# Query weights loaded by groups of four heads instead of whole at the start, with x, w1 and the output in the matching layout: a decode attention and MLP block on one core

## The chip, the core and the metric

The kernel runs on one core of one Trainium2 chip. The core has a matrix engine (TensorE: PE, with its weight loads shown as PEld), a vector engine (DVE), a scalar engine (ACT), GpSimd (POOL), and a synchronisation engine (SP) whose queue issues most of the DMA transfers; 16 DMA engines move the data between HBM and the core's SBUF. The metric is device time in microseconds. The kernel before takes 1960.25 us, the median of three runs that lie between 1960.19 and 1960.85.

## The reference

One token is decoded: layer norm, attention with 32 heads over a cache of 32,768 positions, a residual, a second layer norm, and an MLP. All inputs are bf16.

```
B, Sq, D = 1, 1, 640
H, Sk, Dh = 32, 32768, 192        # Dff = 1536
q = (x @ wq).reshape(B, Sq, H, Dh)                      # wq: 640 x 6144
scores = einsum("bhqd,bhkd->bhqk", q, k_cache) * Dh ** -0.5
p = softmax(scores)
o = einsum("bhqk,bhkd->bhqd", p, v_cache)
A = o.reshape(B, Sq, H * Dh) @ wo                       # wo: 6144 x 640

h  = x + A(layernorm(x))
h2 = h + relu(layernorm(h) @ w1) @ w2                   # w1: 640 x 1536, w2: 1536 x 640
```

The two caches are 403 MB each, wq and wo 7.9 MB each, w1 and w2 2.0 MB each. Every byte is read once.

## The kernel before

**Streaming the caches.** For each head, K and V are loaded in four pieces of 8,192 positions. A piece is a tile of 128 partitions with 64 consecutive positions in each, so each partition receives one row of 24,576 bytes (64 x 192 x 2). K tiles come from kpool and V tiles from vpool, with three buffers each. All these loads are issued on SP's queue (load_part, line 128), in the order of the program; an issue waits until the tile's buffer has been read for the last time. The last piece of the last head is cut into three loads (40, 16 and 8 positions per partition) to shorten the end; the very last K piece takes a wo buffer and the very last V piece a tile of its own, v_end.

**A chunk.** Each piece is worked on in chunks of 32 positions per partition, eight chunks to a head (the index c). Of a chunk's positions, 12 or 16 are scored on DVE (multiply with the spread query, line 287, and sum, line 290). The other 20 or 16 are scored on PE: transposes(g) turns K (line 252) and ACT copies it out of PSUM (line 256), and scores_pe(g) multiplies with the query as columns (line 267). ACT takes the exponentials (lines 272 and 300). pv(g-1) multiplies the chunk before with V, into one PSUM tile for the whole head (line 317). The order on each engine is the order in which the program is written (a manual schedule); around the chunks it fits, by the value of c, the loads of the next pieces (the even c), a load of wo for two heads (c = 1), the finishing of the head before (den_mm, den_rec, o_scale, o_turn at c = 0 and 1), the projection of the last pair of heads (project, line 363, c = 2) and the query of the next head (q_spread, c = 5).

**The query.** wq is loaded ahead of everything, in three loads (load_wq, line 108): two of them borrow a vpool tile and one a kpool tile. The contraction index is split as (p c): partition p holds the five rows 5p to 5p + 4 of wq, whole, so the rows that are moved are 24,576 bytes (two of wq's rows) or 12,288 bytes. Behind them stand, on SP's queue, K and V of the first piece, the first wo load and K of the second piece. q_rows() (line 213) then computes the queries of all heads in 12 blocks of 512 columns, five products each, into q_all; the buffers taken by wq are free when it has ended. Per head, q_spread copies its 192 values from q_all to a row (line 219), spreads them over the partitions by a product with ones (line 221), and makes the columns for scores_pe (line 227).

**The layout of x, h and the output.** They follow wq's split: x is loaded as 128 partitions of five consecutive values (x_b, line 98, on ACT's queue). project and the second product of the MLP (line 435) write the same layout, so they take every fifth column of wo and w2 as weights (n:D:DT). w1 is loaded in the same split, in rows of 15,360 bytes, and its product takes every twelfth column (line 428). The output y is written as 128 rows of five values (line 440).

**The end.** After the last loads of K and V come those of w1 and w2 (load_w, line 146). Then the last head is finished, projected, added to x, normalised, and goes through the MLP.

Of the kernel before, what the change touches and what calls it, by code (L numbers as in the profile page):

```python
# [13 lines left out]
def kernel(  # L14
# [12 lines left out]
    nc = tc.nc  # L27
    P = nc.NUM_PARTITIONS

    Bsz, Sq, D = A_x.shape  # L30
    _, H, Sk, Dh = A_k_cache.shape
    HDh = H * Dh
# [7 lines left out]
    FT = Dff // P  # L40
    JL = 64
    J = 32
    assert Sk % (P * JL) == 0 and 2 * Dh == 3 * P and H % 2 == 0 and HDh % 512 == 0

# [24 lines left out]
    const = ctx.enter_context(tc.tile_pool(name="const", bufs=1))  # L71
    kpool = ctx.enter_context(tc.tile_pool(name="kpool", bufs=3))
    vpool = ctx.enter_context(tc.tile_pool(name="vpool", bufs=3))
    wop = ctx.enter_context(tc.tile_pool(name="wop", bufs=2))
    qbp = ctx.enter_context(tc.tile_pool(name="qbp", bufs=2))
    tsb = ctx.enter_context(tc.tile_pool(name="tsb", bufs=2))
# [10 lines left out]
    def mm_bank(shape, dtype, name):  # L87
        return mps.tile(shape, dtype, tag="mm", name=name)

    k_hd = A_k_cache.rearrange("b h s d -> (b h) s d")  # L90
    v_hd = A_v_cache.rearrange("b h s d -> (b h) s d")

    wq_view = A_wq.rearrange("(p c) n -> p c n", p=P)
    wo_view = A_wo.rearrange("(g p b) n -> g p b n", p=P, b=3)


    x_b = const.tile([P, DT], bf16)
    nc.scalar.dma_start(out=x_b[:], in_=A_x.rearrange("b s (p c) -> (b s p) c", p=P))

    wq_t = {}  # L100
    wo_t = {}
    kt_t = {}
    vt_t = {}

    def load_wq(pool, tag, c0, c1):
        t = pool.tile([P, JL * Dh], bf16, tag=tag, name=tag)
        v = t[:, 0:(c1 - c0) * HDh].rearrange("p (c n) -> p c n", n=HDh)
        nc.sync.dma_start(out=v, in_=wq_view[:, c0:c1, :])
        for c in range(c0, c1):
            wq_t[c] = v[:, c - c0, :]  # L110

    def load_wo(pr):
        t = wop.tile([P, 3 * D], bf16, tag="wo", name="wo")
        t = t[:].rearrange("p (b n) -> p b n", n=D)
        nc.sync.dma_start(out=t, in_=wo_view[pr])
        wo_t[pr] = t

    def load_part(ld, src, pool, tag, name, parts=None):
        h, k0, jl = loads[ld]
        if ld < len(loads) - 1:  # L120
            t = pool.tile([P, JL * Dh], bf16, tag=tag, name=name)
        elif name == "kt":
            t = wop.tile([P, 3 * D], bf16, tag="wo", name=name)
        else:
            t = v_end
        rows = src[h, k0:k0 + P * jl, :].rearrange("(p j) d -> p (j d)", p=P)
        for j0, j1 in parts or [(0, jl)]:
            nc.sync.dma_start(out=t[:, j0 * Dh:j1 * Dh], in_=rows[:, j0 * Dh:j1 * Dh])
        return t
# [10 lines left out]
    def load_w(name, view, pool, tag, cuts):  # L140
        n, N = view.shape[1], view.shape[2]
        assert n * N <= JL * Dh
        t = pool.tile([P, JL * Dh], bf16, tag=tag, name=tag)
        v = t[:, 0:n * N].rearrange("p (c n) -> p c n", n=N)
        for c0, c1 in zip(cuts[:-1], cuts[1:]):
            nc.sync.dma_start(out=v[:, c0:c1], in_=view[:, c0:c1])
        for c in range(n):
            w_t[name, c] = v[:, c, :]

    assert (JL * Dh) // HDh == 2 and DT == 5  # L150
    load_wq(vpool, "vt", 0, 2)
    load_wq(vpool, "vt", 2, 4)
    load_wq(kpool, "kt", 4, 5)


    ident_b = const.tile([P, P], bf16)
# [16 lines left out]
    o_pair = [[const.tile([2, 2 * Dh], f32, name=f"o_pair{i}_{k}") for k in range(2)] for i in range(2)]  # L173
    attT = aps.tile([P, DT], f32, name="attT")
    x_col = const.tile([P, DT], f32)
    q_all = const.tile([1, HDh], bf16)
    v_end = const.tile([P, chunks[-1][4] * Dh], bf16)

    def layernorm_col(col, tag):
        st = small.tile([P, 2], f32, tag=f"st_{tag}", name="st")  # L180
# [18 lines left out]
        return xn  # L199

    with tc.manual_schedule():
        nc.vector.tensor_copy(out=x_col[:], in_=x_b[:])
        xnT = layernorm_col(x_col, "ln1")

        qb_t = {}
        qm_t = {}

        def q_rows():
            for i in range(HDh // 512):
                qps = tps.tile([P, 4, P], f32, tag="tp", name="tp")  # L210
                qps = qps[:].rearrange("p a b -> p (a b)")[0:1, :]
                for c in range(DT):
                    nc.tensor.matmul(qps, lhsT=xnT[:, c:c + 1], rhs=wq_t[c][:, i * 512:(i + 1) * 512],  # L213
                                     start=(c == 0), stop=(c == DT - 1))
                (nc.vector.tensor_copy if i % 2 else nc.scalar.copy)(out=q_all[0:1, i * 512:(i + 1) * 512], in_=qps)  # L215

        def q_spread(h):
            r = rows_e[h % 2]
            nc.scalar.copy(out=r[0:1, Dh:2 * Dh], in_=q_all[0:1, h * Dh:(h + 1) * Dh])  # L219
            qbps = mm_bank([P, Dh + 12], f32, "qbps")  # L220
            nc.tensor.matmul(qbps[:, 0:Dh], lhsT=ones_row[:], rhs=r[0:1, Dh:2 * Dh], start=True, stop=True)  # L221

            i = Dh
            for b in range(3):
                for e in range(2):
                    for off in ((1 - 0) * Dh + b * (2 * P - Dh), b * (2 * P - Dh)):
                        nc.tensor.matmul(qbps[:, i:i + 1], lhsT=r[0:1, off + e:off + 2 * P:2],  # L227
                                         rhs=ones_row[0:1, 0:1], start=True, stop=True)
                        i += 1
            qb = qbp.tile([P, Dh], bf16, name="qb")  # L230
            nc.scalar.copy(out=qb[:], in_=qbps[:, 0:Dh])
            qm = qbp.tile([P, 12], bf16, name="qm")
            nc.scalar.copy(out=qm[:], in_=qbps[:, Dh:Dh + 12])
            qb_t[h], qm_t[h] = qb, qm
# [6 lines left out]
        def transposes(g):  # L241
            h, c, ld, c0, jc, jp = chunks[g]
            kt = kt_t[ld]
            NB = jp * Dh // (2 * P)

            kT = tsb.tile([P, NBM, 2 * P], bf16, name="kT")
            for b0 in range(0, NB, 4):
                nb = min(4, NB - b0)
                tp = tps.tile([P, 4, P], f32, tag="tp", name="tp")
                for b in range(nb):  # L250
                    off = (c0 + jc - jp) * Dh + (b0 + b) * 2 * P
                    nc.tensor.transpose(out=tp[:, b, :], in_=kt[:, off:off + 2 * P].bitcast(f32), identity=ident_f[:])  # L252
                if g == G - 1:
                    nc.vector.tensor_copy(out=kT[:, b0:b0 + nb, :], in_=tp[:, 0:nb, :].bitcast(bf16))
                else:
                    nc.scalar.copy(out=kT[:, b0:b0 + nb, :], in_=tp[:, 0:nb, :].bitcast(bf16))  # L256
            kT_t[g] = kT
# [101 lines left out]
        def project(pr):  # L359
            oT, wo = oT_t.pop(pr), wo_t.pop(pr)  # L360
            for b in range(3):
                for n in range(DT):
                    nc.tensor.matmul(attT[:, n:n + 1], lhsT=wo[:, b, n:D:DT], rhs=oT[:, b:b + 1],
                                     start=(pr == 0 and b == 0 and n == 0),
                                     stop=(pr == H // 2 - 1 and b == 2 and n == DT - 1), skip_group_check=True)

        load_k(0)
        load_v(0)
        q_rows()
        q_spread(0)  # L370
        for g in range(ENDS[0]):
            h, c, ld, c0, jc, jp = chunks[g]
            if c0 == 0 and g > 0:
                load_k(ld)
                load_v(ld)
            if c == 1 and h % 2 == 0:
                load_wo(h // 2)
            transposes(g)
            if g > 0:
                pv(g - 1)  # L380
            scores_pe(g)
            sc = scores_dve(g)
            if c == 0 and h > 0:
                den_mm(h - 1)
                den_rec(h - 1)
                o_scale(h - 1)
            if c == 1 and h > 0:
                o_turn(h - 1)
            if c == 2 and h > 0 and h % 2 == 0:
                project(h // 2 - 1)  # L390
            if c == 5 and h + 1 < H:
                q_spread(h + 1)
            exp_dve(g, sc)
# [2 lines left out]
            load_k(ld)  # L396
        for ld in range(len(loads) - NEND, len(loads)):
            load_v(ld)
        load_w("w1", B_w1.rearrange("(p c) n -> p c n", p=P), kpool, "kt", [0, DT])
        load_w("w2", B_w2.rearrange("(p f) n -> p f n", p=P), vpool, "vt", [0, FT // 2, FT - 2, FT])  # L400
        transposes(ENDS[0])
        pv(ENDS[0] - 1)
# [29 lines left out]
        yps = ops.tile([P, DT], f32, tag="o_ps", name="yps")  # L432
        for f in range(FT):
            for n in range(DT):
                nc.tensor.matmul(yps[:, n:n + 1], lhsT=w_t["w2", f][:, n:D:DT], rhs=h1T[:, f:f + 1],  # L435
                                 start=(f == 0 and n == 0), stop=(f == FT - 1 and n == DT - 1),
                                 skip_group_check=True)
        y = small.tile([P, DT], bf16, tag="y", name="y")
        nc.vector.tensor_add(out=y[:], in0=h_col[:], in1=yps[:])
        nc.sync.dma_start(out=out.rearrange("b s (p c) -> (b s p) c", p=P), in_=y[:])  # L440


# [28 lines left out]
```

## Time and profile before

| quantity | value |
|---|---|
| median of three runs | 1960.25 us |
| the profiled execution, its own time | 1960.25 us |
| its span, first to last instruction | 1958.4 us |
| HBM read | 824.97 MB, 421 GB/s over the span |
| mean granted TensorE clock | 0.861 of full speed |
| PE / DVE / ACT busy, share of the span | 82% / 81% / 50% |
| queue q1 (loads issued by SP), share of 16 DMA engines | 98.8% |
| first chunk's first product with K, start | 37.24 us |
| x landed, after its issue | 10.2 us |
| out landed, after its issue | 2.8 us |

How to read it. Times within the execution are counted from its first instruction. Busy shares are averages over the whole span. The groups of instructions give an engine's line, operation, tiles and shapes, then the total busy time and the mean time of one in ns, and then the engine's idle time ahead of them with what ended it. In the waits, a line names the engine and line that waited, what it waited for, the total, the number of waits and the longest. In the stretches, a line gives the stretch, its length, the busy time of PE, PEld, DVE, ACT and POOL with the number of instructions, the granted TensorE clock, the busy share of the DMA engines and the rate in GB/s. The chain of waits is followed back from the last instruction: at each step to what released it, or to the instruction ahead of it on its engine.

### The profile page before, as it was taken

The page shows a single profiled execution, that of the slowest core. Times are in us where ns is not written, and L with a number is a line of the kernel's source. Part 1 is how long each engine was busy: PE and PEld are TensorE (multiplying, and loading weights), DVE is VectorE, ACT ScalarE, POOL GpSimd, SP SyncE. Part 2 cuts the span into 40 slices and gives each one's busy share as a digit, 9 for nine tenths or more (in the row PEclk, how much of TensorE's full clock was granted, in tenths as well). Part 3 has the DMA queues.
Part 4 walks back from the last instruction along what each step waited for, and adds up shares of the span by engine and source line. Part 5 has one row for each costly group of instructions (what it writes and reads, how often), then busy time and mean ns, then how long its engine had stood idle before and what let it go on. Part 6 is the DMA issues. An engine that isn't in the chain of part 4 may idle for free.

```text
span 1958.4 us, 35516 instructions
## 1 busy us (share of the span) xinstructions
PE 1603.5 (82%) x15578; PEld 1098.4 (56%) x15578; DVE 1583.7 (81%) x913; ACT 984.2 (50%) x2068; POOL 0.7 (0%) x6
## 2 busy tenths in 40 slices
PE   5888888888888888888887888788788887887887
PEld 2555555555555555555565655556555555555555
DVE  3897887888788888888887888788888878788885
ACT  2554545545555545454554545454555545455553
POOL 0000000000000000000000000000000000000000
PEclk9888888888888888898888888888888888889888
DMA  9999999999999999999999999999999999999996
GB/s 408 427 430 427 429 428 428 429 427 429 427 429 428 429 429 428 429 427 428 428 429 428 429 426 429 428 429 428 428 429 427 429 425 429 425 426 429 422 418 241
DMA packets 41338, 827.25 MB, mean 422 GB/s; under 512 B 4832, under 2 KB 4832, under 8 KB 8032
## 3 DMA queue, kind: packets, MB, share of 16 engines
q1 hardware_dynamic: 41040, 824.99, 98.8%
q8 instruction: 122, 2.00, 0.4%
q14 instruction: 32, 0.26, 0.0%
q10 hardware_dynamic: 144, 0.00, 0.0%
HBM read 824.97 MB, written 0.00 MB: 421 GB/s over the span
## 4 chain that ended last, share of the span: by engine, by line
DMA 70%; DVE 19%; PE 9%; issue 1%; ACT 0%; DVEq 0%; SPq 0%; ACTq 0%
DMA kt<-in_A_k_cache_dram 69%; DVE pr L287 11%; DVE sc L290 8%; PE o_ps L317 4%; PE tp L252 3%; DMA kt<-in_A_wq_dram 1%; PE sp L267 1%; PE tp L213 1%; DVE o_pair L340 0%; ACT kT L256 0%; PE h1ps L428 0%; PE den L323 0%; PE yps L435 0%; DVE rec L329 0%; DVE rec L330 0%
## 5 line engine op out<-in xcount | busy, mean ns | idle before, releaser
L287 DVE TENSOR_TENSOR pr<-kt,qb 128x1536 f32<-128x1536 bf16 (+1 forms) x384 | 775.4, 2019 | 225.1 <-DMA kt<-in_A_k_cache_dram 216.7
L256 ACT COPY kT<-tp 128x1024 bf16<-128x1024 bf16 (+1 forms) x898 | 816.5, 989 | 277.4 <-PE tp L252 270.6
L252 PE MATMUL tp<-ident_f,kt 128*128 128x128 f32 x3462 | 585.4, 336 | 305.4 <-DMA kt<-in_A_k_cache_dram 294.4
L290 DVE TENSOR_REDUCE sc<-pr 128x8 f32<-128x1536 f32 (+1 forms) x384 | 774.0, 2016 | 31.9 <-DVE pr L287 1.4
L252 PEld LDWEIGHTS tp<-ident_f,kt 128*128 128x128 f32 x3462 | 508.6, 176 | 322.8 <-issue 298.6
L317 PE MATMUL o_ps<-vt,pB 128*2 128x384 bf16 x2304 | 483.3, 362 | 3.1 <-DMA vt<-in_A_v_cache_dram 3.1
L317 PE MATMUL o_ps<-vt,pA 128*2 128x384 bf16 x1788 | 333.7, 327 | 0.0
L317 PEld LDWEIGHTS <-pB 128*2 128x2 bf16 x2308 | 189.0, 90 | 248.4 <-issue 137.4
L272 ACT ACTIVATE pB<-sp 128x20 bf16<-128x20 f32 (+2 forms) x258 | 47.8, 185 | 484.9 <-PE sp L267 484.9
L267 PEld LDWEIGHTS <-kT 128*128 128x128 bf16 x6924 | 192.7, 97 | 85.5 <-issue 84.1
L317 PEld LDWEIGHTS <-pA 128*2 128x2 bf16 x1788 | 151.5, 85 | 145.5 <-issue 7.6
L267 PE MATMUL sp<-qm,kT 128*128 128x2 bf16 x6924 | 214.7, 164 | 1.1 <-ACT kT L256 1.1
L300 ACT ACTIVATE pA<-sc 128x12 bf16<-128x12 f32 (+2 forms) x257 | 53.9, 210 | 115.0 <-DVE sc L290 114.9
L329 DVE TENSOR_REDUCE rec<-den 128x1 f32<-128x20 f32 x32 | 5.7, 179 | 68.7 <-PE den L323 68.7
L272 ACT ACTIVATION_READ_ACCUMULATOR pB<-sp 128x1 f32 x258 | 50.2, 195 | 0.0
L300 ACT ACTIVATION_READ_ACCUMULATOR pA<-sc 128x1 f32 x257 | 49.0, 190 | 0.0
L341 ACT ACTIVATE o_pair<-o_ps,rec 2x192 f32<-2x192 f32 x32 | 18.8, 589 | 32.7 <-DVE o_pair L340 32.7
L353 PE MATMUL oT_ps<-ident_f,o_pair 2*128 2x1 f32 x192 | 24.1, 247 | 0.9 <-DVE o_pair L340 0.6
L227 PEld LDWEIGHTS <-row_e 1*128 1x128 bf16 x384 | 13.6, 92 | 17.9 <-issue 17.9
L353 PEld LDWEIGHTS oT_ps<-ident_f,o_pair 2*128 2x128 f32 x192 | 22.6, 186 | 1.6 <-DVE o_pair L340 1.0
L221 PE MATMUL qbps<-row_e,ones_row 1*128 1x192 bf16 x32 | 7.6, 238 | 18.4 <-ACT row_e L219 17.2
L215 DVE CAST q_all<-tp 1x512 bf16<-1x512 f32 x6 | 4.1, 678 | 20.0 <-PE tp L213 20.0
(55 smaller groups left out, 169.7 us busy)
## 6 DMA issues: line engine op xcount, KB each, us to landing
kt<-in_A_k_cache_dram SPq DMA_DIRECT2D x127, 3072.0 KB, 33.1
vt<-in_A_v_cache_dram SPq DMA_DIRECT2D x127, 3072.0 KB, 30.5
wo<-in_A_wo_dram SPq DMA_DIRECT2D x16, 480.0 KB, 31.2
vt<-in_A_wq_dram SPq DMA_DIRECT2D x2, 3072.0 KB, 13.5
kt<-in_A_k_cache_dram SPq DMA_DIRECT2D x1, 1920.0 KB, 26.4
vt<-in_A_v_cache_dram SPq DMA_DIRECT2D x2, 960.0 KB, 19.2
kt<-in_B_w_dram SPq DMA_DIRECT2D x1, 1920.0 KB, 17.7
kt<-in_A_wq_dram SPq DMA_DIRECT2D x1, 1536.0 KB, 20.2
```

Source lines behind the costliest of these rows:

```text
L213: nc.tensor.matmul(qps, lhsT=xnT[:, c:c + 1], rhs=wq_t[c][:, i * 512:(i + 1) * 512], start=(c == 0), stop=(c == DT - 1))
L227: nc.tensor.matmul(qbps[:, i:i + 1], lhsT=r[0:1, off + e:off + 2 * P:2], rhs=ones_row[0:1, 0:1], start=True, stop=True)
L252: nc.tensor.transpose(out=tp[:, b, :], in_=kt[:, off:off + 2 * P].bitcast(f32), identity=ident_f[:])
L256: nc.scalar.copy(out=kT[:, b0:b0 + nb, :], in_=tp[:, 0:nb, :].bitcast(bf16))
L267: nc.tensor.matmul(sp[:, 4 * i + b:4 * i + b + 2], lhsT=kT[:, 3 * i + b, e:2 * P:2], rhs=qm[:, 4 * b + 2 * e:4 * b + 2 * e + 2], start=(i ...
L272: nc.scalar.activation(out=pB[:, 0:JP], in_=sp[:, 0:JP], func=F.Exp, scale=SCALE, accum_out=dsums[:, h, 2 * c + 1:2 * c + 2])
L287: nc.vector.tensor_tensor(out=pr[:, 0:j1 - j0, :], in0=kt[:, (c0 + j0) * Dh:(c0 + j1) * Dh].rearrange("p (j d) -> p j d", d=Dh), in1=qb[:] ...
L290: nc.vector.reduce_sum(out=sc[:, j0:j1], in_=pr[:, 0:j1 - j0, :], axis=mybir.AxisListType.X)
L300: nc.scalar.activation(out=pA[:, 0:JD], in_=sc[:, 0:JD], func=F.Exp, scale=SCALE, accum_out=dsums[:, h, 2 * c:2 * c + 1])
L317: nc.tensor.matmul(o[:], lhsT=p, rhs=vt[:, (c0 + j) * Dh:(c0 + j + 2) * Dh], start=first, stop=last)
L341: nc.scalar.activation(out=dst[1][:, p0:p1, :], in_=src[:, 1], func=F.Copy, scale=s[0:2, 1:2])
L353: nc.tensor.matmul(ps[:, b:b + 1], lhsT=src[i][:, b * P:(b + 1) * P], rhs=ident_f[0:2, i:i + 1], start=(i == 0), stop=(i == 1))
```

## The change

wq is no longer loaded whole ahead of everything. It is loaded in eight loads of four heads each (QG = 4) into a pool of its own with two buffers: the first ahead of the loop, each other one at c = 3 of the third head of the group before. The contraction index is split as (c p): partition p holds the rows p, 128 + p, 256 + p, 384 + p and 512 + p, and of each the 768 columns of the group. So a load has 640 rows of 1,536 bytes. q_rows(h) computes one head's query, five products of 192 columns, at c = 4 of the head before, and ACT copies it from PSUM into the row that q_spread reads; q_all and the copy in q_spread go.

The layout of x, h and the output follows the new split. x is loaded as five rows of 128 values and turned on PE. project and the second MLP product take 128 consecutive columns as weights. w1 is loaded in 640 rows of 3,072 bytes; its product still takes every twelfth column. The output is turned on PE, copied, and written as five rows of 128 values. The last K piece and the last V piece use buffers of wq's pool. The SBUF that all this takes is the same.

```diff
+    wqp = ctx.enter_context(tc.tile_pool(name="wqp", bufs=2))
-    wq_view = A_wq.rearrange("(p c) n -> p c n", p=P)
+    wq_view = A_wq.rearrange("(c p) n -> p c n", p=P)
-    x_b = const.tile([P, DT], bf16)
-    nc.scalar.dma_start(out=x_b[:], in_=A_x.rearrange("b s (p c) -> (b s p) c", p=P))
+    x_row = const.tile([DT, P], bf16)
+    nc.scalar.dma_start(out=x_row[:], in_=A_x.rearrange("b s (c p) -> (b s c) p", p=P))
-    def load_wq(pool, tag, c0, c1):
-        t = pool.tile([P, JL * Dh], bf16, tag=tag, name=tag)
-        v = t[:, 0:(c1 - c0) * HDh].rearrange("p (c n) -> p c n", n=HDh)
-        nc.sync.dma_start(out=v, in_=wq_view[:, c0:c1, :])
-        for c in range(c0, c1):
-            wq_t[c] = v[:, c - c0, :]
+    def load_wq(gq):
+        t = wqp.tile([P, DT * QG * Dh], bf16, tag="wq", name="wq")
+        t = t[:].rearrange("p (c n) -> p c n", c=DT)
+        nc.sync.dma_start(out=t, in_=wq_view[:, :, gq * QG * Dh:(gq + 1) * QG * Dh])
+        wq_t[gq] = t
...
-        if ld < len(loads) - 1:
-            t = pool.tile([P, JL * Dh], bf16, tag=tag, name=name)
-        elif name == "kt":
-            t = wop.tile([P, 3 * D], bf16, tag="wo", name=name)
+        if ld == len(loads) - 1:
+            pool, tag, size = wqp, "wq", DT * QG * Dh
         else:
-            t = v_end
+            size = JL * Dh
+        t = pool.tile([P, size], bf16, tag=tag, name=name)
...
-    load_wq(vpool, "vt", 0, 2)
-    load_wq(vpool, "vt", 2, 4)
-    load_wq(kpool, "kt", 4, 5)
+    load_wq(0)
...
-        nc.vector.tensor_copy(out=x_col[:], in_=x_b[:])
+        xps = mm_bank([P, DT], bf16, "xps")
+        nc.tensor.transpose(out=xps[:], in_=x_row[:], identity=ident_b[0:DT, 0:DT])
+        nc.vector.tensor_copy(out=x_col[:], in_=xps[:])
...
-        def q_rows():
-            for i in range(HDh // 512):
-                qps = tps.tile([P, 4, P], f32, tag="tp", name="tp")
-                qps = qps[:].rearrange("p a b -> p (a b)")[0:1, :]
-                for c in range(DT):
-                    nc.tensor.matmul(qps, lhsT=xnT[:, c:c + 1], rhs=wq_t[c][:, i * 512:(i + 1) * 512],
-                                     start=(c == 0), stop=(c == DT - 1))
-                (nc.vector.tensor_copy if i % 2 else nc.scalar.copy)(out=q_all[0:1, i * 512:(i + 1) * 512], in_=qps)
+        def q_rows(h):
+            gq, hh = divmod(h, QG)
+            wq = wq_t[gq]
+            qps = mm_bank([1, Dh], f32, "qps")
+            for c in range(DT):
+                nc.tensor.matmul(qps[:], lhsT=xnT[:, c:c + 1], rhs=wq[:, c, hh * Dh:(hh + 1) * Dh],
+                                 start=(c == 0), stop=(c == DT - 1))
+            r = rows_e[h % 2]
+            nc.scalar.copy(out=r[0:1, Dh:2 * Dh], in_=qps[:])
         def q_spread(h):
             r = rows_e[h % 2]
-            nc.scalar.copy(out=r[0:1, Dh:2 * Dh], in_=q_all[0:1, h * Dh:(h + 1) * Dh])
...
-                    nc.tensor.matmul(attT[:, n:n + 1], lhsT=wo[:, b, n:D:DT], rhs=oT[:, b:b + 1],
+                    nc.tensor.matmul(attT[:, n:n + 1], lhsT=wo[:, b, n * P:(n + 1) * P], rhs=oT[:, b:b + 1],
...
-        q_rows()
+        q_rows(0)
...
+            if c == 3 and h % QG == QG - 2 and h + 2 < H:
+                load_wq(h // QG + 1)
...
+            if c == 4 and h + 1 < H:
+                q_rows(h + 1)
...
-        load_w("w1", B_w1.rearrange("(p c) n -> p c n", p=P), kpool, "kt", [0, DT])
+        load_w("w1", B_w1.rearrange("(c p) n -> p c n", p=P), kpool, "kt", [0, DT])
...
-                nc.tensor.matmul(yps[:, n:n + 1], lhsT=w_t["w2", f][:, n:D:DT], rhs=h1T[:, f:f + 1],
+                nc.tensor.matmul(yps[:, n:n + 1], lhsT=w_t["w2", f][:, n * P:(n + 1) * P], rhs=h1T[:, f:f + 1],
...
-        y = small.tile([P, DT], bf16, tag="y", name="y")
-        nc.vector.tensor_add(out=y[:], in0=h_col[:], in1=yps[:])
-        nc.sync.dma_start(out=out.rearrange("b s (p c) -> (b s p) c", p=P), in_=y[:])
+        y_col = small.tile([P, DT], f32, tag="y_col", name="y_col")
+        nc.vector.tensor_add(out=y_col[:], in0=h_col[:], in1=yps[:])
+        ytp = mm_bank([DT, P], f32, "ytp")
+        nc.tensor.transpose(out=ytp[:], in_=y_col[:], identity=ident_f[:])
+        y_row = small.tile([DT, P], bf16, tag="y_row", name="y_row")
+        nc.vector.tensor_copy(out=y_row[:], in_=ytp[:])
+        nc.sync.dma_start(out=out.rearrange("b s (c p) -> (b s c) p", p=P), in_=y_row[:])
```

More of the change, by code (lines that the diff above doesn't have):

```diff
@@ L42 @@
     J = 32
-    assert Sk % (P * JL) == 0 and 2 * Dh == 3 * P and H % 2 == 0 and HDh % 512 == 0
+    QG = 4
+    assert Sk % (P * JL) == 0 and 2 * Dh == 3 * P and H % QG == 0 and H % 2 == 0
     full = [(JL, [(J, 20), (J, 16)])] * (Sk // (P * JL))
@@ L103 @@
     vt_t = {}
-    def load_wq(pool, tag, c0, c1):
-        t = pool.tile([P, JL * Dh], bf16, tag=tag, name=tag)
-        v = t[:, 0:(c1 - c0) * HDh].rearrange("p (c n) -> p c n", n=HDh)
-        nc.sync.dma_start(out=v, in_=wq_view[:, c0:c1, :])
-        for c in range(c0, c1):
-            wq_t[c] = v[:, c - c0, :]
+    def load_wq(gq):
[3 more added lines that the diff above has]
+        wq_t[gq] = t
     def load_wo(pr):
-        t = wop.tile([P, 3 * D], bf16, tag="wo", name="wo")
-        t = t[:].rearrange("p (b n) -> p b n", n=D)
-        nc.sync.dma_start(out=t, in_=wo_view[pr])
+        t = wop.tile([P, 3, D], bf16, name="wo")
+        nc.sync.dma_start(out=t[:], in_=wo_view[pr])
         wo_t[pr] = t
@@ L148, in load_w @@
             w_t[name, c] = v[:, c, :]
-    assert (JL * Dh) // HDh == 2 and DT == 5
-    load_wq(vpool, "vt", 0, 2)
-    load_wq(vpool, "vt", 2, 4)
-    load_wq(kpool, "kt", 4, 5)
+    load_wq(0)
     ident_b = const.tile([P, P], bf16)
@@ L175 @@
     x_col = const.tile([P, DT], f32)
-    q_all = const.tile([1, HDh], bf16)
-    v_end = const.tile([P, chunks[-1][4] * Dh], bf16)
     def layernorm_col(col, tag):
@@ L248, in transposes @@
                 nb = min(4, NB - b0)
-                tp = tps.tile([P, 4, P], f32, tag="tp", name="tp")
+                tp = tps.tile([P, 4, P], f32, name="tp")
                 for b in range(nb):
```

## The prediction

> **What bounds the kernel now.** I read the page first, then the waits of the SP queue, the stretches, the end of the chain of waits and the groups of instructions. The page (engine: busy us, share, instructions; 40 slices; queues):
>
> ```profile
> span 1958.4 us, 35516 instructions
> ...
> PE 1603.5 (82%) x15578; PEld 1098.4 (56%) x15578; DVE 1583.7 (81%) x913; ACT 984.2 (50%) x2068; POOL 0.7 (0%) x6
> ...
> DMA  9999999999999999999999999999999999999996
> GB/s 408 427 430 427 429 428 428 429 427 429 427 429 428 429 429 428 429 427 428 428 429 428 429 426 429 428 429 428 428 429 427 429 425 429 425 426 429 422 418 241
> ...
> q1 hardware_dynamic: 41040, 824.99, 98.8%
> q8 instruction: 122, 2.00, 0.4%
> ```
>
> Every slice but the last moves data at one rate while no engine passes 82%: the load stream of queue q1 is the bound. Next, whether that stream can run dry (releaser: total us, times, longest; then the issues with KB and us from issue to landing):
>
> ```profile
> SPq L128 <- PE o_ps L317: 1172.8, 125, 12.4
> SPq L128 <- DVE pr L287: 602.0, 126, 12.1
> ```
>
> ```profile
> kt<-in_A_k_cache_dram SPq DMA_DIRECT2D x127, 3072.0 KB, 33.1
> vt<-in_A_v_cache_dram SPq DMA_DIRECT2D x127, 3072.0 KB, 30.5
> ...
> vt<-in_A_wq_dram SPq DMA_DIRECT2D x2, 3072.0 KB, 13.5
> ...
> kt<-in_A_wq_dram SPq DMA_DIRECT2D x1, 1536.0 KB, 20.2
> ```
>
> SP waits for free tiles, but a load needs 33 us to land where its own 3.15 MB take 7.3 us at 428 GB/s: over three other loads stand queued ahead of it, so SP's waits cost nothing. The stretches (width, busy by engine, clock, DMA share, GB/s) show that the 16 DMA engines are not equal:
>
> ```profile
> 900.00:1000.00 100.00, 84.54 (x823) 57.88 (x822) 82.11 (x47) 52.37 (x111) 0.00 (x0) 0.86 1.00 428
> ```
>
> ```profile
> 1909.00:1912.00 3.00, 2.77 (x37) 1.56 (x35) 2.96 (x2) 1.65 (x4) 0.00 (x0) 1.00 0.64 268
> ...
> 1939.00:1943.00 4.00, 3.01 (x24) 1.62 (x21) 0.87 (x3) 0.68 (x3) 0.00 (x0) 1.00 0.49 201
> 1943.00:1946.00 3.00, 2.00 (x25) 1.94 (x25) 0.56 (x5) 1.45 (x2) 0.00 (x0) 0.95 0.40 160
> ```
>
> At 1909 us six have run out of queued rows (0.64 of 16 busy); at 1939 us half of them are done for good, and the other half run on to about 1946. In the trace's packet records the packets of one wo load are all out within 1.8 us at the start and spread over 22.3 us in the last wo load: some engines fall behind by 1.55 us in every 118. The 122 instruction packets (1.07 us each) account for 16 us of it if they fall on 8 engines, 15 each. A load has landed when its slowest engine has, so those engines set the time. Per engine, by packet intervals as below (24-KB rows at their mean, 0.916): K and V 2032 x 0.916 = 1861.5, wq 18.2, wo 18.9, the last small loads 23.9; with the lag of 22.3 and the start at 1.4 us that is 1946.2. The account closes: the slow engines never rest.
>
> The end (start us, us, what):
>
> ```profile
> 1899.93 26.36 DMA kt<-in_A_k_cache_dram
> ...
> 1944.75 0.74 PE attT L363 x15
> ...
> 1948.00 3.70 PE h1ps L428 x60
> 1951.70 0.02 issue
> 1951.73 0.19 ACT h1T L431
> 1951.91 0.04 issue
> 1951.96 2.54 PE yps L435 x60
> 1954.49 0.02 issue
> 1954.52 0.16 DVE y L439
> ```
>
> After the last large K load (1926.3) 28 us of PE, ACT and DVE follow. So the time is: the stream up to that K load, plus this tail. The profiled execution took 1960.25 us, the very median of the three; 1.85 us lie around its span.
>
> **The change part by part.** *wq.* Removed: three loads ahead of everything, 24-KB and 12-KB rows, 256 + 128 packets. Added: eight loads of 0.98 MB, 640 rows of 1,536 B each, 5,120 packets; one stands first, seven in the third head of a group (c = 3). The bytes are equal, so only the cost per packet counts. From the packet records:
>
> ```
> bytes   packets  median ns
> 24576   32768    915
> 12288   128      460
> 7680    384      291
> 3840    2048     151
> 3072    256      121
> 2560    128      102
> ```
>
> A line through these has 36.9 ns per KB (decimal) and 7.5 ns fixed; but a packet starts some 3.5 ns before the one ahead of it ends (the engines' summed packet times exceed the elapsed time, 1.004 of it among 24-KB rows, 1.02 in the first wo load), so some 4 ns are real. 1,536 B is below any row there: 56.7 + 4 = 60.7 ns. Per engine now 16 x 0.9115 + 8 x 0.456 = 18.2 us, then 320 x 0.0607 = 19.4: **+1.2**. Bounds: 0 (no fixed cost), +2.3 with the whole 7.5 ns, and, from the one kind of packet that runs far off the line, instruction fetch (16,384 B in 1,073 ns), 100 ns, 32.0 us, +13.8. I take the line: wo's rows are nearest.
>
> Here a rule can be weighed. The row: 3,840-B packets run at 407 GB/s over 16 engines, 24-KB ones at 430. The Trainium skill, "DMA: Bandwidth & Descriptors", Specifications, has line rate from 512 B on; wq would then cost 0 and the sum be 1960.7. The same page, in "Anatomy of one DMA", fits 2.0 us plus bytes to each DMA and under "Bandwidth" wants 1 MiB or more in each, which speaks against eight loads of 0.94 MiB: five more would be +10, or 1971.9. The share of 1.00 says that queued loads hide such a fixed part.
>
> *SP's order.* Each wq load stands behind a V issue and ahead of the next K issue, which waits some 4.8 us (602.0/126) for DVE anyway; an issue of five times the rows may hold SP for 5 x 0.43 = 2.1 us, hidden by that wait. The slot is free: its last reader ran four heads before. Landing at 33 us is in time for q_rows nine chunks, 66 us, later. The last K and V piece take wq slots last read in heads 26 and 30; no wait is added.
>
> *Start.* K0 no longer stands behind 7.9 MB, so the first chunk can begin near 12 us, not 37.2. That gains nothing: the stream was not held up by that delay (share 0.95 to 1.05 up to 50 us). Lost may be some of the first load, should its 640 rows be generated slowly: -0.3 (small first packets arrive sooner) to +2.1 (SP's issue); I take **+0.3**, since one 128-row issue already hid behind streaming. x as 5 rows plus a PE transpose lies beside the first loads: 0.
>
> *q by heads.* The 60 products before the loop (15 us of PE on the chain, after 20 us of waiting for wq) become five per head at c = 4, at most 5 x 0.238 (L221) = 1.2 us of PE; PE idles 294.4 us waiting for K, 9.2 per head. Without that cover it would cost 31 x 1.2 = 37 us. ACT's copy (0.33, L219) becomes one from PSUM (0.32, L231's row). On ACT the wait for these products delays exp_dve, which waits for DVE (114.9 us) anyway. Some 200 more PE instructions are one more instruction packet over 8 engines: **+0.1**.
>
> *w1* in 3,072-B rows: 40 x 117.5 against 8 x 569.5 ns per engine, +0.15, behind the last K and V. It landed at 1942.9 and is wanted at 1948.0: 0. w2 behind it lands near 1948 and its last rows are read after 1953.
>
> *Tail.* project and w2 read their weights in one run instead of every fifth column. The groups:
>
> ```profile
> L267 PEld LDWEIGHTS <-kT 128*128 128x128 bf16 x6924 | 192.7, 97 | 85.5 <-issue 84.1 <-ACT kT L256 1.4
> L363 PEld LDWEIGHTS <-wo 128*128 128x128 bf16 x240 | 10.9, 130 | 0.2 <-issue 0.2
> L428 PEld LDWEIGHTS <-kt 128*128 128x128 bf16 x60 | 3.9, 166 | 1.4 <-issue 1.4
> L435 PEld LDWEIGHTS <-vt 128*128 128x128 bf16 x60 | 2.6, 131 | 0.3 <-issue 0.3
> ```
>
> Step 2 (L267) issues a pair every 31 ns, at half clock too; step 5 every 42 to 48; step 12 (L428, unchanged) every 61. With 31 ns, L435 loses 60 x 11 = 0.7 and the last project 15 x 17 = 0.25. Added: a transpose of y and a copy. DVE to PE to DVE costs 0.9 in ln2 (1945.95 to 1946.85, two small products); 128 moving columns at half clock may add 0.1: +1.0. Five output rows for 128: at most -0.2 of 2.8, taken as 0. Tail: **0.0** (-0.7 to +0.8).
>
> Sum: 1.2 + 0.3 + 0.1 + 0.0 = +1.6 us: **1961.9**.
>
> **The rivals.** (a) *1,536-B packets fall off the line*, because an engine can't keep enough reads under way. At 100 ns, the fetch row, 1974. It decides, that is the kernel is slower by over 0.2% (3.9 us, about what a measurement of it can tell from no change), from 68 ns on: 320 x 7.3 ns more than forecast. For it: no row is that small. Against: from 24 KB down to 2.5 KB the line bends by 2 ns at most. (b) *The rows cost nothing and the tail gains*: 0 + 0 + 0.1 - 0.5, near 1959.8. For it: half the fixed cost is already seen to overlap. Against: wo's rate of 407. (c) *The first load starves the stream*: +2.1 with the full 7.5 ns, 1960.25 + 2.3 + 2.1 + 0.1 + 0.5 = 1965.3. (d) *Over 3.9 us faster*: would need rest on the slow engines, and the account leaves only the 1.4 us at the start.
>
> **How the numbers follow.** Forecast 0.60 (own range 1960.5 to 1963.6), (a) 0.16, (b) 0.12, (c) 0.09, (d) 0.03. Slower: all of (a), most of (c): 0.24. Faster: (d) 0.03. Same: 0.73. The range starts at (b)'s value, 1959.8, and ends at 1968.0 (wq packets at some 80 ns), inside (a).
>
> **What would show it.** Right: q1's share near 98.8% again, packets of 1,536 B near 64 ns, slices holding 425 or more, chunk one near 12 us, L435 at 1.9 us, the last large K load landing 1.5 us later. Wrong: slices with wq loads (every fourth head, 235 us apart) below 415 GB/s, or a DMA share under 0.95 in the first 10 us.

## The result

The changed kernel takes 1947.41 us (median of 6 runs, 1946.88 to 1947.87) against 1960.44 us for the kernel before in the same series: a ratio of 0.9934, 95% interval 0.9921 to 0.9947. It is 13.0 us, or 0.66%, faster. Forecast were 1961.9 us, a range of 1959.8 to 1968.0 and a chance of 0.03 for "faster". The prediction is wrong, in sign and by far more than its range.

The page of the changed kernel, with the lines that answer to those shown of the kernel before:

```profile
span 1946.1 us, 35719 instructions
...
PE 1598.2 (82%) x15680; PEld 1100.3 (57%) x15680; DVE 1579.6 (81%) x908; ACT 985.0 (51%) x2062; POOL 0.7 (0%) x6
...
DMA  9999999999999999999999999999999999999996
GB/s 406 433 431 429 430 432 430 431 430 430 432 429 432 430 431 431 433 426 433 433 429 431 428 431 432 431 430 431 430 430 430 431 429 431 430 430 428 430 421 248
...
q1 hardware_dynamic: 46234, 824.99, 99.1%
q8 instruction: 123, 2.02, 0.4%
```

The engines' busy times are the same within 6 us, the DMA engines are as full as they were, and the bytes are equal. What differs is the rate at full share: 428 to 429 GB/s in most slices before, 430 to 432 now. The same stretch in both kernels (before first, then the changed one; length, busy times of PE, PEld, DVE, ACT, POOL, clock, DMA share, GB/s):

```profile
600.00:1000.00 400.00, 334.96 (x3243) 231.83 (x3242) 329.40 (x185) 205.61 (x431) 0.00 (x0) 0.85 1.00 428
```

```profile
600.00:1000.00 400.00, 334.19 (x3241) 229.69 (x3240) 327.76 (x185) 204.07 (x425) 0.00 (x0) 0.85 1.01 431
```

Three GB/s in 428 are 0.7%, the whole of the result. This stretch still holds two of the loads of wq, at 628 and 865 us. The one from 900 to 1000 us holds none; the prediction shows it for the kernel before, at 428 GB/s, and in the changed kernel it reads:

```profile
900.00:1000.00 100.00, 83.50 (x809) 57.29 (x807) 82.77 (x47) 51.90 (x109) 0.00 (x0) 0.86 1.00 431
```

So the same 24-KB rows move faster, with no load of wq among them. The packet records say it row by row: of the 32,768 rows of 24,576 bytes before, 17,503 took 915 ns, 6,911 took 922, and only 1,165 took 912; the mean is 919.6. In the changed kernel 32,225 of 32,512 took 912; the mean is 914.5. The 122 instruction packets took 1,068 ns on average before and 933 now, and wo's rows, 149 to 159 ns before, take 149.

The end of the chain of waits in the changed kernel (start us, us, what):

```profile
1870.32 32.98 DMA kt<-in_A_k_cache_dram
...
1934.42 0.53 PE attT L358 x15
...
1937.26 3.61 PE h1ps L427 x60
...
1941.13 1.75 PE yps L434 x60
...
1942.90 0.17 DVE y_col L438
1943.08 0.04 issue
1943.12 0.39 PE ytp L440
1943.51 0.02 issue
1943.53 0.28 DVE y_row L442
```

The last full K piece landed at 1903.3 where it landed at 1914.3 before: 11 of the 13 us were won in the stream, ahead of the tail.

### The profile page after: what moved, and what is told of

The parts are those of the page before. It is cut to its first block, busy times and chain, and to the rows that moved or that the text cites. A ratio compares the mean times of both kernels' runs of the same rounds, so it can differ in the third digit from the quotient of the medians.

```text
span 1946.1 us, 35719 instructions
## 1 busy us (share of the span) xinstructions
PE 1598.2 (82%) x15680; PEld 1100.3 (57%) x15680; DVE 1579.6 (81%) x908; ACT 985.0 (51%) x2062; POOL 0.7 (0%) x6
## 3 DMA queue, kind: packets, MB, share of 16 engines
q1 hardware_dynamic: 46234, 824.99, 99.1%
## 4 chain that ended last, share of the span: by engine, by line
DMA 69%; DVE 21%; PE 9%; issue 1%; ACT 0%; DVEq 0%; SPq 0%; ACTq 0%
DMA kt<-in_A_k_cache_dram 69%; DVE pr L282 12%; DVE sc L285 8%; PE o_ps L312 4%; PE tp L247 3%; PE sp L262 1%; DVE o_pair L335 0%; PE den L318 0%; PE h1ps L427 0%; DVE rec L324 0%; DVE rec L325 0%; ACT kT L251 0%; PE yps L434 0%; DVEq L285 0%; PE oT_ps L348 0%
## 5 line engine op out<-in xcount | busy, mean ns | idle before, releaser
L312 PE MATMUL o_ps<-vt,pB 128*2 128x384 bf16 x2308 | 477.9, 358 | 0.3 <-ACT kT L251 0.3
L208 PE MATMUL qps<-wq,xn_ln 128*1 128x192 bf16 x160 | 18.7, 248 | 2.5 <-DMA wq<-in_A_wq_dram 2.5
L335 DVE TENSOR_SCALAR o_pair<-o_ps,rec 2x192 f32<-2x192 f32 x32 | 17.4, 544 | 2.8 <-PE o_ps L312 1.7
L211 ACT CAST row_e<-qps 1x192 bf16<-1x192 f32 x32 | 9.8, 308 | 9.7 <-PE qps L208 9.7
```

The lines of the kernel that those rows point to most:

```text
L208: nc.tensor.matmul(qps[:], lhsT=xnT[:, c:c + 1], rhs=wq[:, c, hh * Dh:(hh + 1) * Dh], start=(c == 0), stop=(c == DT - 1))
L312: nc.tensor.matmul(o[:], lhsT=p, rhs=vt[:, (c0 + j) * Dh:(c0 + j + 2) * Dh], start=first, stop=last)
L335: nc.vector.tensor_scalar_mul(out=dst[0][:, p0:p1, :], in0=src[:, 0], scalar1=s[0:2, 1:2])
```

## The experiments

**Two theories.** The compiled programs give the place of each tile in a partition of SBUF. Before, the K and V tiles begin at 45,088 and the five steps of 24,576 behind it: 32 bytes beyond a multiple of 256. In the changed kernel they begin at 29,952, a multiple of 256. Theory A: the place of the K and V tiles sets the time of their rows, and the change moved them by accident. Theory B: the way wq is loaded makes the gain (no late first chunk, no borrowed K and V tiles). The first four kernels move tiles without touching the order of any work.

**The kernel before, all tiles 32 bytes on**

```diff
     x_col = const.tile([P, DT], f32)
+    const.tile([P, 16], bf16, name="pad")
```

> The kernel before with 32 unused bytes per partition added behind x_col, so that the K and V tiles begin at a multiple of 64 bytes in a partition of SBUF (45120 instead of 45088); nothing else is changed, wq still comes first in three loads. Theory A (the gain is the position of the K and V tiles: rows that land 32 bytes off a multiple of 64 take longer, 915 to 922 ns in the packet records of before against 912 in those of the changed kernel, 2032 such rows per DMA engine x 5.1 ns of mean difference = 10.4 us, and about 2 us from shorter instruction packets, 1068 to 933 ns x 15): 1948 us, 24-KB rows at 912 ns. Theory B (the gain is the way wq is loaded: no late start of the first chunk, no borrowed K and V tiles): 1960.4 us, rows at 915 to 922 ns as before.

Measured: 1958.05 us against 1960.0 for the kernel before, ratio 0.9989 (0.9980 to 0.9999). A small gain, far from 1948: a multiple of 64 is not enough. Both theories, as written, missed. 24-KB rows fell by 1 ns only (most at 914 and 921).

**The changed kernel, all tiles 32 bytes on**

```diff
     x_col = const.tile([P, DT], f32)
+    const.tile([P, 16], bf16, name="pad")
```

> The changed kernel with the same 32 bytes added, so that its K and V tiles begin 32 bytes off a multiple of 64 (29984 instead of 29952). Theory A: what the changed kernel gained by its tiles' position goes, 1947.4 + 12.4 = 1959.8 us, rows at 915 to 922 ns. Theory B: no change, 1947.4 us.

Measured: 1961.1 us, ratio to the kernel before 1.0005 (0.9996 to 1.0015). With 32 unused bytes the gain is gone, and theory B with it: wq is loaded here as in the changed kernel. Rows are back at 915 and 922 ns, and so is the rate:

```profile
600.00:1000.00 400.00, 326.48 (x3205) 226.30 (x3204) 323.37 (x183) 200.53 (x423) 0.00 (x0) 0.85 1.00 427
```

**The kernel before, K and V tiles 32 bytes on, those behind them 64**

```diff
+    const.tile([P, 16], bf16, name="pad")
...
     vpool = ctx.enter_context(tc.tile_pool(name="vpool", bufs=3))
+    gap = ctx.enter_context(tc.tile_pool(name="gap", bufs=1))
+    gap.tile([P, 16], bf16, name="gap")
```

> The kernel before with 32 unused bytes ahead of the K and V tiles and 32 more behind them: K and V tiles at a multiple of 64 bytes, and the tiles behind them (wo, qb, qm, kT, pr, the probabilities) still 32 bytes off one, as in the kernel before. Theory A (DMA writes of K and V alone): within 1 us of the kernel before with all tiles shifted, 1948 us; wo's 3,840-byte rows stay at 149 to 155 ns. Rival C (the engines read and write kT, pr and the rest faster there): 1960.4 us, or a part of the way; against it stands that DVE, ACT and PE were no faster in the changed kernel (2019, 989, 336 and 337 ns).

Measured: 1957.79 us, ratio 0.9988 (0.9979 to 0.9998), the same as with everything moved (1958.05). So the place of K and V matters, and that of kT, pr and the rest doesn't show; but this shift gains only 2 us, so the test is weak and is made again below.

**The changed kernel, all tiles 64 bytes on**

```diff
+    const.tile([P, 32], bf16, name="pad")
```

> The changed kernel with 64 unused bytes added: K and V tiles at a multiple of 64 bytes but of no more (30016, where it was 29952, a multiple of 256). Theory A with a period of 64 bytes: 1947.4 us, rows at 912 ns. If the period is 128 or 256 bytes: slower, up to 1959.8 us.

Measured: 1959.2 us, ratio 0.9995 (0.9986 to 1.0005). A multiple of 64 is not enough here either; the changed kernel's 29,952 is a multiple of 256. The next four test a period of 256.

**The kernel before, only K and V at multiples of 256**

```diff
+    const.tile([P, 112], bf16, name="pad")
...
     vpool = ctx.enter_context(tc.tile_pool(name="vpool", bufs=3))
+    gap = ctx.enter_context(tc.tile_pool(name="gap", bufs=1))
+    gap.tile([P, 144], bf16, name="gap")
```

> The kernel before with 224 unused bytes ahead of the K and V tiles and 288 behind them: K and V tiles (and wq and w1, w2, which use them) begin at multiples of 256 bytes (45312); every tile behind them moves by 512 bytes, so that it stands as before to any smaller power of two. wq still comes first in three loads. Theory A, now with a period of 256 bytes (shifts of 32 and 64 cost the changed kernel 13.7 and 11.8 us, and shifting the kernel before from 32 to 64 gained 2): 24-KB rows at 912 ns throughout, 1960.0 - 13.7 + 0.5 for wo, which stays at 149 to 155 ns = 1947. Theory B' (the gain needs the way wq is loaded as well): 1958 or more.

Measured: 1947.67 us, ratio 0.9936 (0.9921 to 0.9951). This is the decisive run: wq first, x, w1, projection and output as in the kernel before, every tile behind K and V in the same place modulo 512, and the whole gain is there. (q_all, v_end and the two normalised inputs, which stand between the unused bytes and K, move by 224 bytes too; the run that moves V alone, below, leaves them where they were and gains as well.) 32,412 of 32,768 rows take 912 ns, instruction packets 934 ns, wo's rows 149 ns (2,029 of 2,048) although they stayed 32 bytes off, where 149 to 155 was expected, and the stretch runs at the changed kernel's rate:

```profile
600.00:1000.00 400.00, 330.98 (x3246) 225.23 (x3245) 330.51 (x187) 204.99 (x432) 0.00 (x0) 0.87 1.00 431
```

**The changed kernel, all tiles 128 bytes on**

```diff
+    const.tile([P, 64], bf16, name="pad")
```

> The changed kernel with 128 unused bytes added, K and V tiles at 128 beyond a multiple of 256. Theory A with a period of 256 bytes: near the shift of 64, 1959 us, most rows at 914 ns or more. If a period of 128 is enough: 1947.4 us and 912 ns.

Measured: 1958.49 us, ratio 0.9992 (0.9983 to 1.0001). A multiple of 128 is not enough: 8,396 of 32,512 rows at 912 ns, most of the others at 913 to 921.

**The kernel before, only K at multiples of 256**

```diff
+    const.tile([P, 112], bf16, name="pad")
...
     kpool = ctx.enter_context(tc.tile_pool(name="kpool", bufs=3))
+    gap = ctx.enter_context(tc.tile_pool(name="gap", bufs=1))
+    gap.tile([P, 144], bf16, name="gap")
```

> The kernel before with 224 unused bytes ahead of the K tiles and 288 between K and V: only the K tiles at multiples of 256, V and all else as before. Theory A, if each off row costs its own time: half of the rows lose it, 1960.0 - 6.6 = 1953.4 us, and the 24-KB rows fall into two equal parts, 912 and 914 to 922 ns. If the cost comes from something shared (instruction packets, one slow port): near 1947 or near 1960 us.

Measured: 1952.11 us, ratio 0.9960 (0.9945 to 0.9974): 8.1 us won, not 6.6. Three quarters of the rows, 24,613, take 912 ns, where half have their place right.

```profile
600.00:1000.00 400.00, 333.28 (x3239) 228.74 (x3238) 330.27 (x187) 203.25 (x432) 0.00 (x0) 0.85 1.01 430
```

**The kernel before, K, V and all behind them at multiples of 256**

```diff
+    const.tile([P, 112], bf16, name="pad")
```

> The kernel before with 224 unused bytes ahead of all that follows x_col: K and V as in the run that moved these alone, and wo at a multiple of 256 too (149 ns for all its rows, 128 x 3.6 ns = 0.5 us less per DMA engine). Theory A: 1946.5 us, and against the changed kernel at 1947.4 this leaves the true price of the change: 1,536-B rows of wq (+1.2 to +2.3) less what its tail gains (about 1 us).

Measured: 1947.32 us, ratio 0.9935 (0.9918 to 0.9951). Moving wo too makes 0.35 us between the medians, which these runs can't tell from none. One line of unused bytes in the kernel before gives the time of the changed kernel.

The last four were run beside each other to price what the change does apart from moving tiles.

**The changed kernel with wq whole and first**

```diff
-    wqp = ctx.enter_context(tc.tile_pool(name="wqp", bufs=2))
...
-    load_wq(0)
+    load_wq(vpool, "vt", 0, 2)
+    load_wq(vpool, "vt", 2, 4)
+    load_wq(kpool, "kt", 4, 5)
...
-        q_rows(0)
+        q_rows()
...
-            if c == 3 and h % QG == QG - 2 and h + 2 < H:
-                load_wq(h // QG + 1)
...
-            if c == 4 and h + 1 < H:
-                q_rows(h + 1)
```

The fence leaves out load_wq, q_rows, q_all and the copy in q_spread, and the last K and V pieces: all of them are as in the kernel before.

> The changed kernel with one part of the change undone: wq whole and ahead of everything again, in three loads into K and V tiles and with the queries of all heads computed before the loop. The split of the contraction index stays that of the changed kernel, so wq's rows are 12,288 bytes (640 of them). K, V and wo tiles begin at multiples of 256 bytes. If 5,120 rows of 1,536 bytes cost what I worked out (+1.2 us) and the early first chunk is worth nothing: 1946.2 us, 1.2 less than the changed kernel. If loading wq by groups is a gain of its own (first chunk at 13 instead of 37 us): 1948 us or more.

Measured: 1946.19 us (1945.43 to 1946.99), ratio 0.9929 (0.9917 to 0.9942). It is at the first of the two values, so loading wq by groups shows no gain of its own.

**The kernel before, only V at multiples of 256**

```diff
     kpool = ctx.enter_context(tc.tile_pool(name="kpool", bufs=3))
+    gap = ctx.enter_context(tc.tile_pool(name="gap", bufs=1))
+    gap.tile([P, 112], bf16, name="gap")
     vpool = ctx.enter_context(tc.tile_pool(name="vpool", bufs=3))
+    gap2 = ctx.enter_context(tc.tile_pool(name="gap2", bufs=1))
+    gap2.tile([P, 144], bf16, name="gap2")
```

> The kernel before with only the V tiles (with the wq and w2 loads that use them) at multiples of 256 bytes, K tiles and all else as before. If the costs of K rows and V rows add up: 1960.2 - (12.6 - 8.1) = 1955.7 us. If one off kind of row also slows its neighbours, so that either alone gives the same: 1952 us.

Measured: 1952.13 us, ratio 0.9960 (0.9946 to 0.9974), the same as with K alone. The costs do not add: either half of the rows gives 8 us, the second half 4.6 more. 23,488 rows take 912 ns, far more than the 16,512 that are in place (V's and those of the two wq loads into V tiles).

**The two references of this series**

> The changed kernel as it is, once more, to stand beside the runs of this series on one chip: 1947.4 us.

> The kernel before with K, V and wo tiles at multiples of 256 bytes, once more beside the others: 1947.3 us; less what project, w2 and the output gain (some 1.1 us by the traces), the changed kernel with wq first is to stand at 1946.2.

Measured: 1947.59 us (1947.25 to 1947.75) for the changed kernel, 1946.84 (1946.65 to 1947.75) for the kernel before with its tiles moved, beside 1959.94 for the kernel before. With the changed kernel that loads wq whole and first, the change comes apart: moving the tiles, 1946.84 - 1959.94 = -13.1; layout of x, w1, projection and output (and wq's rows all at 12,288 bytes), 1946.19 - 1946.84 = -0.65; wq in groups of four heads, 1947.59 - 1946.19 = +1.4. The last two are differences of medians of five runs that spread over 0.5 to 1.6 us, so their sizes are good to about a microsecond, and that the layout gains at all is not certain. Their sum, +0.75, was +0.1 in the earlier series (1947.41 against 1947.32). The changed kernel with wq whole and first has the lowest median of all, 0.7% under the kernel before.

The table gathers the packet records (times in ns; "off" is the place of the K and V tiles modulo 256):

```
kernel                          off       median us  24-KB rows: mean, at 912    instruction packets
before                          32        1960.2     919.6    1165 of 32768      1068
before, 32 on                   64        1958.1     919.0    3180               1069
before, K V 32 on               64        1957.8     918.9    3174               1066
before, K at 256                K 0 V 32  1952.1     916.5   24613               1056
before, V at 256                K 32 V 0  1952.1     916.6   23488               1056
before, K and V at 256          0         1947.7     914.9   32412                934
before, all at 256              0         1947.3     915.0   32397                932
changed                         0         1947.4     914.5   32225 of 32512       933
changed, 32 on                  32        1961.1     919.6     945               1069
changed, 64 on                  64        1959.2     918.9    2875               1072
changed, 128 on                 128       1958.5     918.4    8396               1071
changed, wq first               0         1946.2     914.5   32267                930
```

2048 rows per DMA engine, 4.7 ns each in the mean (919.6 - 914.9), are 9.6 us; 15 instruction packets, 0.135 us shorter, 2.0 us. Together 11.6 of the 12.6 us that moving K and V brought.

## Why the prediction was wrong, by its own steps

**What bounds the kernel: right.** The load stream sets the time, and the slow engines never rest. That is why a fraction of a per cent on each row went into the result undiminished. The signs named for the terms came true as well: q1's share is 99.1%, 1,536-B rows take 65 ns, all slices but the first and the last two hold 426 GB/s or more, the first chunk starts at 13.4 us. Only the last one failed: the K loads end 11 us earlier, not 1.5 us later.

**The step that failed** is the costing of x: "x as 5 rows plus a PE transpose lies beside the first loads: 0." The edit was costed as work and not as storage. x's tile held 5 values per partition, which take 32 bytes of each partition with padding; it now holds 128, 256 bytes. The tiles that go, q_all and v_end, are 12,288 and 3,072 bytes, together 60 x 256, and change nothing modulo 256. So K and V moved from 45,088 by 224 - 15,360 to 29,952: x's 224 bytes alone put them on a multiple of 256. The run with 224 unused bytes, and no other part of the change, shows it: 1947.32 us, where this term was taken as 0. That "the SBUF that all this takes is the same", as said of the change above, holds only roughly: wo begins 224 bytes further on, and these are the ones that count.

**The account that hid it.** The table of packets in the prediction took medians and a line through the sizes, and gave 24-KB rows one price, 915 ns. The account by engine then needed their mean, 0.916 us after the overlap, to close. That gap was the sign: wo's rows had a second value beside 149, and 24-KB rows lay between 912 and 922. Rows of one size with several durations in one steady stream ask for a reason. (That instruction packets lay "far off the line" was no such sign: at 933 ns they still do.) With one price for every row, rival (d), over 3.9 us faster, was dismissed with "would need rest on the slow engines"; but a faster row wins time without any rest.

**The terms of the sum.** The wq term was right in kind, and in size as far as the runs tell: +1.2 was forecast with 1,536-B rows near 64 ns, and the records have 65 ns. The +1.4 us between runs holds the start and the extra instruction packet too, for which 0.3 and 0.1 were forecast. Of the start the records show 0.1 to 0.3 us: after 100 us the changed kernel had moved 41.67 MB, the kernel before with its tiles moved 41.73 and 41.78 in its two traces. Rival (a), packets that fall off the line, is answered: they don't. Its reason, too few reads under way, was not tested. The rule of the Trainium skill weighed there ("DMA: Bandwidth & Descriptors", Specifications: line rate from 512 B on) would have had 0; here the 1,536-B rows run at 378 GB/s over 16 engines by their 65 ns, those of 24 KB at 431 by their 912. Its 2 us for each load, which that page fits to transfers issued from GpSimd while these are issued by SP, gave +10 as an estimate; the runs show nothing of that size. The early first chunk was worth nothing, as forecast: it began at 13.4 us, 24 us earlier, and wq first still has the lower median. q by heads hid itself: 248 ns for each of the 160 products, and PE still waits 325 us for K.

The tail's groups (line, engine, operation, tiles, shapes, count; busy us, mean ns; idle ahead):

```profile
L358 PEld LDWEIGHTS <-wo 128*128 128x128 bf16 x240 | 7.2, 96 | 0.2 <-issue 0.2
L427 PEld LDWEIGHTS <-kt 128*128 128x128 bf16 x60 | 3.7, 156 | 1.4 <-issue 1.4
L434 PEld LDWEIGHTS <-vt 128*128 128x128 bf16 x60 | 1.8, 104 | 0.3 <-issue 0.3
```

The second MLP product fell from 2.54 to 1.75 us (forecast 1.9) and the last project from 0.74 to 0.53 (forecast 0.5). Turning y cost 0.74 (forecast 1.0). Mis-sized was the output: from the end of the last DVE instruction to the end of the span the kernel before takes 3.7 us and the changed one 2.3, so five rows in place of 128 won 1.4 us, where I had bounded it by 0.2, without a row behind the bound, and taken 0. SP's wait for it (first the kernel before, then the changed one):

```profile
SPq L466 <- DMA out_dram<-y: 2.3, 1, 2.3
```

```profile
SPq L469 <- DMA out_dram<-y_row: 0.8, 1, 0.8
```

About 0.8 us less shows ahead of it in this trace: from the landing of the last full K piece to the start of the last project, 30.4 us before and 31.1 now. It goes with the clock that PE was granted as that piece landed (0.52 here, in the column ahead of the DMA share), and not with the change:

```profile
1902.00:1906.00 4.00, 2.56 (x12) 2.59 (x13) 2.56 (x1) 1.69 (x4) 0.00 (x0) 0.52 0.96 378
```

In the four us after the landing and the four after those, the granted clock was 0.50 and 0.75 in this trace; in the kernel before it was 0.58 and 0.95; in the changed kernel's other trace 0.61 and 0.96, and there the whole way takes 30.5 us; in the last trace of the kernel before with its tiles moved 0.50 and 0.80, and 31.1 us. So single executions of one kernel differ by some 0.7 us in this part alone.

Without the tiles' place, then, my sum of +1.6 stands against a measured +0.1 to +0.75 us. The terms that were costed came out within 1.5 us, most of it the output's gain, and the largest effect was not on the list.

## What to carry to other kernels

In a kernel that is bound by loads, list the place of every streamed tile in its partition before and after an edit: a small tile that grows, shrinks or goes moves all that is allocated behind it, and here 224 bytes were worth 13 us. Put streamed tiles at multiples of 256 bytes on purpose, ahead of small tiles or with padding, so that edits elsewhere can't move them. When packets of one size show several durations, find out which of them differ in place before taking a median.

## What the runs showed of the hardware

Rows of 24,576 bytes that land at a multiple of 256 bytes in a partition take 912 ns almost without exception; at 32, 64 or 128 beyond, most take 913 to 922. The whole kernel loses 13.5, 11.6 and 10.9 us by these offsets against the changed kernel's 1947.6. The period of 256 is read from two pairs: tiles 32 and 288 bytes beyond a multiple of 512 have the same mean row (919.6 ns both), and so have those 64 and 320 beyond (919.0 and 918.9). All K and V tiles that were in place stood 256 beyond a multiple of 512; a multiple of 512 itself was not run.

The Trainium skill, "DMA: Bandwidth & Descriptors", section "How a descriptor splits into AXI transactions", says that a transfer is split into pieces of 256 bytes from 256-byte boundaries, and that one which starts off a boundary carries beats of 32 bytes that are of no use. It tells this of the bytes that are read; here the place where they are written was moved. The period of 256 agrees with the runs. The size does not: counted in such beats, an estimate from that page, 32 bytes off would cost one beat in 768, 0.13% or 2.4 us, and 128 off four times that, 9.7 us; measured were 13.5 and 10.9 us, so the cost falls where the estimate rises.

What makes up the time of an off row is open in part. The cost isn't an equal price per row, since K alone or V alone at the right place saves 8 us and both together 12.6. The packet records show where the long rows stand. An engine's packets can be followed, because each starts 3 to 4 ns before the one ahead of it ends, or 2 to 3 ns behind it where a new load begins. A load gives an engine eight rows. In the run with V alone in place, the first five of an engine's eight K rows take 912 ns and the last two or three are longer; the V row behind them is longer too, though it is in place, and the others are back at 912. Directly behind wo's rows, which are off as well, all eight K rows are longer; wo's own rows take 149 ns there (2,030 of 2,048). With K alone in place V's rows show the same, and of wo's rows, now behind rows of V that are off, only 964 take 149. In the kernel before no row in place breaks the sequence, and hardly any row takes 912. So the time of a row depends on the off rows that stand ahead of it on its engine, and not on its own place alone.

Whether the engines beside it count too is open. The engines drift apart in the course of the kernel: with K alone in place, longer rows run on up to all 16 engines at once from 100 to 160 us, and on ten at most from 600 to 700 us. The share of rows at 912 ns does not follow this, it is 73 to 75% in each 100 us up to 1,600; but with V alone in place it varies from 67 to 74%, and is 84% in the next 100. Packets of another queue, the instructions, are slowed by 14% while K and V are both off (1,068 against 934 ns) and by 13% while one of them is (1,056). Why the first off rows go free, no run shows.
